# Query blocks outermost, 1536-column exponentials, one gelu block per query block and a planned instruction order in an attention-plus-MLP kernel

## The chip, the cores and the metric

The kernel runs on one core of a Trainium2 chip. The metric is the device time in microseconds (us) of one execution. Every kernel was run several times beside the kernel before on the same chip. The profiled execution's span is about 2 us shorter than its timed run.

## The reference, cut to what matters

```python
x = A_x                                   # (1, 2048, 512), bf16
xn = layernorm(x)                         # no gain, no bias
# attention: 32 heads of 16 columns, no mask
q, k, v = split(xn @ wqkv)
p = softmax(q @ k.T * 16 ** -0.5)         # 32 heads x 2048 x 2048
a = (p @ v) @ wo
# MLP, on a layernorm of the layernorm
y = layernorm(xn)
h = gelu_tanh(y @ w1 + b1)                # 2048 x 1792
out = x + a + (h @ w2 + b2)
```

Softmax needs 32 x 2048 x 2048 = 134 million exponentials. Over 128 lanes that is 1,048,576 columns for ScalarE, whichever way they are cut.

Of the kernel before, what the change touches and what calls it, by code (L numbers as in the profile page):

```python
# [12 lines left out]
ALU = mybir.AluOpType  # L13
# [5 lines left out]
SYNC_DEP = mybir.DependencyInfo(mybir.DependencyClass.Sync, mybir.DependencyReason.DATA)  # L19
# [7 lines left out]
BOUND_INFL = 0.505  # L27
L_MIN = 1e-25
L_MAX = 1e6
GELU_C = float(np.sqrt(2.0 / np.pi))  # L30
_DBG = os.environ.get("PSM_DBG")


class _Jobs:

    NPRIO = 4

    def __init__(self, held):
        self.q = [[] for _ in range(self.NPRIO)]
        self.credit = 0.0  # L40
        self.held = held
        self.sticky = None
        self.activity = 0.0
        self.paused = set()

    def add(self, gen, prio):
        self.q[prio].append(gen)
        return gen

    def _first(self):  # L50
        if self.sticky is not None:
            return self.sticky
        for q in self.q:
            if q and q[0] not in self.paused:
                return q
        return None

    def step(self):
        q = self._first()
        if q is None:  # L60
            return None
        g = q[0]
        try:
            c = next(g)
        except StopIteration:
            q.pop(0)
            c = 0
            assert not self.held(), "job finished while holding the misc bank"
        self.sticky = q if self.held() else None
        if c == "pause":  # L70
            assert self.sticky is None
            self.paused.add(g)
            c = 0
        if isinstance(c, tuple):
            c, a = c
        else:
            a = c
        self.activity += a
        return c

    def run(self, budget):
        self.credit = min(self.credit, 0.0) + budget
        self.activity = 0.0
        self.paused = set()
        while self.credit > 0.0:
            c = self.step()
            if c is None:
                break
            self.credit -= c
        return self.activity  # L90

    def pending(self, gen):
        return any(gen in q for q in self.q)

    def finish(self, gen):
        while self.pending(gen):
            self.paused = set()
            self.step()

    def drain(self):  # L100
        while True:
            self.paused = set()
            if self.step() is None:
                break
        self.credit = 0.0
# [3 lines left out]
def kernel(  # L109
# [11 lines left out]
    dense_per_round: float = 2.4,  # L121
    pe_fill: float = 3.0,
# [13 lines left out]
    NKT = S // P  # L136
    TQ = QW // P
    assert S % QW == 0 and D % P == 0 and F % P == 0 and H % HS == 0
    SW = HS * DH
    NCH = QW // 32  # L140

    const = ctx.enter_context(tc.tile_pool(name="const", bufs=1))
    big = ctx.enter_context(tc.tile_pool(name="big", bufs=1))

    def gate_on(mm, gate):
        if gate is not None:
            tc.add_manual_dep(mm.ins, gate.ins.name, ORDER_DEP, reason="order gate")

# [3 lines left out]
    seln = const.tile([P, P], BF, name="seln")  # L152
    selr = const.tile([P, P], BF, name="selr")
    eps_t = const.tile([P, 1], F32, name="eps_t")
    onescol = const.tile([P, 1], F32, name="onescol")
    onescol2 = const.tile([P, 1], F32, name="onescol2")
    okmin = const.tile([P, 1], F32, name="okmin")
    ones_f = const.tile([P, 1], F32, name="ones_f")
    r2m1 = const.tile([P, NT], F32, name="r2m1")
    b1_sb = const.tile([P, FC], BF, name="b1_sb")  # L160
    b2_sb = const.tile([1, D], BF, name="b2_sb")
    flag_i = const.tile([1, 1], I32, name="flag_i")
    wq_pad = big.tile([P, JC, H, 32], BF, name="wq_pad")
    wk_pad = big.tile([P, JC, H, 32], BF, name="wk_pad")
    wv_sb = big.tile([P, JC, D], BF, name="wv_sb")
    wo_pad = big.tile([P, NS, D], BF, name="wo_pad")
    w1_sb = big.tile([P, JC, F], BF, name="w1_sb")
    w2_sb = big.tile([P, FC, D], BF, name="w2_sb")
    va_bufs = [big.tile([P, NKT, HS, 32], BF, name=f"va{i}") for i in range(2)]
    acc = big.tile([P, NT, D], F32, name="acc")  # L170
    kt0p = big.tile([P, S], BF, name="kt0p")
    kmx0 = const.tile([P, NQT], F32, name="kmx0")
    xnT_c = [big.tile([P, JC, QW], BF, name=f"xnT{tq}") for tq in range(NQT)]
    r2m1b = big.tile([P, S], BF, name="r2m1b")
# [3 lines left out]
    G = 4  # L178

    def load_acc(gate=None):  # L180
        for t0_ in range(0, NT, G):
            d_ = nc.gpsimd.dma_start(acc[:, t0_:t0_ + G, :], xv[:, t0_:t0_ + G, :])
            if gate is not None:
                tc.add_manual_dep(d_.ins, gate.ins.name, SYNC_DEP, reason="x first")

    with tc.tile_pool(name="start", bufs=1) as st, \
            tc.tile_pool(name="startw", bufs=3) as stw, \
            tc.tile_pool(name="pst", bufs=3, space=PSUM) as pst, \
            tc.tile_pool(name="psk", bufs=4, space=PSUM) as psk, \
            tc.tile_pool(name="psw", bufs=1, space=PSUM) as psw:  # L190
        x_sb = st.tile([P, NT, D], BF, name="x_sb")
        for gi_, t0_ in enumerate(range(0, NT, G)):
            (nc.sync if gi_ % 2 == 0 else nc.scalar).dma_start(
                x_sb[:, t0_:t0_ + G, :], xv[:, t0_:t0_ + G, :])
        with nc.allow_non_contiguous_dma(reason="tiny bias load"):
            nc.scalar.dma_start(b1_sb[:], B_b1.rearrange("(fc p) -> p fc", p=P))
        nc.scalar.dma_start(b2_sb[:], B_b2[None, :])

        make_identity(nc, ident_bf[:])
        nc.vector.memset(ones_bf[:], 1.0)  # L200
        nc.vector.memset(zeros_bf[:], 0.0)
        nc.vector.memset(ones_f[:], 1.0)
        nc.vector.memset(seln[:], 0.0)
        nc.vector.memset(selr[:], 0.0)
        for j in range(HS):
            nc.vector.memset(seln[32 * j:32 * j + DH, 32 * j + DH:32 * j + DH + 1], 1.0)
            nc.vector.memset(selr[32 * j:32 * j + 1, 32 * j + DH:32 * j + DH + 2], 1.0)
        nc.vector.memset(eps_t[:], LN_EPS)
        nc.vector.memset(okmin[:], 1.0)
        pm0 = psw.tile([P, 1], F32, tag="w", name="pm0")  # L210
        nc.tensor.matmul(pm0[:], lhsT=selr[:], rhs=ones_bf[:, 0:1], start=True, stop=True)
        nc.vector.tensor_copy(onescol2[:], pm0[:])
        for j in range(HS):
            nc.vector.memset(selr[32 * j:32 * j + 1, 32 * j + DH + 1:32 * j + DH + 2], 0.0)
        pm1 = psw.tile([P, 1], F32, tag="w", name="pm1")
        nc.tensor.matmul(pm1[:], lhsT=selr[:], rhs=ones_bf[:, 0:1], start=True, stop=True)
        nc.vector.tensor_copy(onescol[:], pm1[:])
        for jc in range(JC):
            nc.vector.memset(wk_pad[:, jc, :, DH:32], 0.0)
            nc.gpsimd.memset(wq_pad[:, jc, :, DH:32], 0.0)  # L220
        for va_i in va_bufs:
            nc.gpsimd.memset(va_i[:].rearrange("p k j r -> p (k j r)"), 0.0)
            nc.gpsimd.memset(va_i[:, :, :, DH:DH + 1], 1.0)

        stats = st.tile([P, NT, nc.vector.BN_STATS_DIM], F32, name="stats")
        mv = st.tile([P, NT, nc.vector.BN_AGGR_DIM], F32, name="mv")
        sd1 = st.tile([P, NT], F32, name="sd1")
        sd2 = st.tile([P, NT], F32, name="sd2")
        r1 = st.tile([P, NT], F32, name="r1")
        v2 = st.tile([P, NT], F32, name="v2")  # L230
        assert D <= nc.vector.BN_STATS_FMAX
        gate_stat = None
        for t in range(NT):
            nc.vector.bn_stats(out=stats[:, t, :], in_=x_sb[:, t, :])  # L234
            ag = nc.vector.bn_aggr(out=mv[:, t, :], in_=stats[:, t, :])
            if t == min(NT - 1, 2 * G):
                gate_stat = ag
        wqk = st.tile([P, JC, 2 * D], BF, name="wqk")
        wo_v = A_wo.rearrange("(s j r) c -> j r s c", j=HS, r=DH)
        loads = [(wqk[:, :, D:2 * D], wv_view[:, :, D:2 * D]),  # L240
                 (wqk[:, :, 0:D], wv_view[:, :, 0:D]),
# [3 lines left out]
        for dst_, src_ in loads:  # L245
            d_ = nc.sync.dma_start(dst_, src_)
            tc.add_manual_dep(d_.ins, gate_stat.ins.name, SYNC_DEP, reason="x first")
# [637 lines left out]
```

## The kernel before: the parts that the change and the argument touch

Heads are taken in groups of four ("sets", 8 of them). The loop has the set outermost, then the query block of 512 (`qt`), then the key tile of 128 (`kt`). Each step makes four score tiles (one per head, one PSUM bank each) and two exponentials of two banks.

```python
rounds = [(s, qt, kt) for s in range(NS) for qt in range(NQT) for kt in range(NKT)]
# [cut]
def emit_act(k):
    p_t = ppool.tile([P, 2, QW], BF, tag="p", name=f"p{k}")
    acts[k] = nc.scalar.activation(p_t[:].rearrange("p a b -> p (a b)"),
                                   sct[k][:].rearrange("p a b -> p (a b)"),
                                   AF.Exp, scale=float(DH) ** -0.5)      # 1024 columns
# [cut]
for r in range(NR):
    emit_act(2 * r)
    emit_qk(r + 1)                  # TensorE: next four score tiles
    emit_pv(r - 1)                  # TensorE: P.V of the round before
    done = jobs.run(dense_per_round)        # a budget of other matmuls
    emit_fill(nfill)                # zero matmuls that keep the clock up
    emit_act(2 * r + 1)
```

The other work (projections, MLP, output sums) comes as generator "jobs" that are stepped within a budget in each round, so its place in TensorE's stream follows from the rounds.
The gelu is made of a tanh on ScalarE and three VectorE passes per 512 columns; the division by the softmax sum is done on VectorE with 32x32 transposes; the sums over the sets are kept in an f32 accumulator in SBUF. Both square roots of the layernorms are taken before the stream begins:

```python
nc.scalar.activation(out=sd1[:], in_=mv[:, :, 1], func=AF.Sqrt, bias=eps_t[:], scale=1.0)
# [cut]
nc.scalar.activation(out=sd2[:], in_=v2[:], func=AF.Sqrt, bias=eps_t[:], scale=1.0)
# [cut]
nc.scalar.activation(out=uv, in_=uv, func=AF.Tanh, scale=GELU_C)      # per chunk of 512
```

## Time and profile before

| | before |
|---|---|
| time, median of 4 runs | 1040.63 us (1040.37 to 1042.9) |
| span of the profiled run, mean granted clock | 1038.8 us, 0.986 |
| ScalarE busy | 988.0 us, 95% |
| TensorE busy | 835.0 us, 80% |
| first exponential | 40.2 us |
| last exponential to the end | 12.8 us |

### The profile page before, as it was taken

Reading aid. Unit: us, or ns where it says so; the run is one execution under the profiler, and the core shown is the slowest. Engines: PE = TensorE matmul, PEld = TensorE weight load, DVE = VectorE, ACT = ScalarE, POOL = GpSimd, SP = SyncE. Lnnn points to the kernel's source line nnn. Section 1 sums busy time; section 2 is a strip of 40 time slices with the busy share of each in tenths; the row PEclk is TensorE's granted clock in tenths of the full one; section 3 lists DMA queues with packets and bytes.
Section 4 is the critical chain, followed back from the end, with each engine's and each line's share of the span. In section 5 each row is a group of like instructions: output and inputs, shape, how many; then the busy total and the mean of one; then the engine's idle time right before and its main releaser. Section 6 shows DMA issues by size and latency. Waiting matters only on the chain.

```text
span 1038.8 us, 15620 instructions
## 1 busy us (share of the span) xinstructions
PE 835.0 (80%) x6085; PEld 251.2 (24%) x6197; DVE 452.5 (44%) x976; ACT 988.0 (95%) x1106; POOL 13.2 (1%) x19
## 2 busy tenths in 40 slices
PE   5778877888778889888778887788888877788885
PEld 2312221222212222222222222122222222222221
DVE  8543894513954413536924259451134432112222
ACT  2799999999999999999999999999999999999995
POOL 5000000000000000000000000000000000000000
PEclk8999999999989999999999999999999999999998
DMA  8800000000000000000000000000000000000000
GB/s 256 210 1 1 2 1 1 1 1 1 1 1 1 2 1 1 1 2 1 1 1 1 2 1 1 1 2 1 1 2 1 1 1 1 1 1 21 21 22 23
DMA packets 12913, 15.22 MB, mean 15 GB/s; under 512 B 2337, under 2 KB 10274, under 8 KB 12834
## 3 DMA queue, kind: packets, MB, share of 16 engines
q1 hardware_dynamic: 6704, 7.87, 2.9%
q0 software_dynamic: 2112, 4.19, 1.2%
q10 hardware_dynamic: 4018, 2.10, 0.7%
q8 instruction: 50, 0.82, 0.3%
q14 instruction: 29, 0.24, 0.1%
HBM read 9.97 MB, written 2.10 MB: 12 GB/s over the span
## 4 chain that ended last, share of the span: by engine, by line
ACT 56%; PE 22%; issue 13%; DVE 7%; DMA 1%; ACTq 0%; SPq 0%; DVEq 0%
ACT p L751 53%; PE sc L741 8%; PE o L768 4%; PE o L804 2%; ACT u L598 2%; PE pk L367 1%; PE pq L406 1%; PE po L626 1%; PE ph L580 1%; PE po L607 1%; DVE stats L234 1%; DVE pre L588 1%; DVE qraw L414 1%; PE pvp L476 1%; DMA x_sb<-in_A_x_dram 0%
## 5 line engine op out<-in xcount | busy, mean ns | idle before, releaser
L751 ACT ACTIVATE p<-sc 128x1024 bf16<-128x1024 f32 x1024 | 958.1, 1138 | 14.6 <-PE sc L741 13.2
L768 PE MATMUL o<-p,va 128*32 128x512 bf16 x2048 | 241.1, 391 | 45.7 <-ACT p L751 43.2
L741 PE MATMUL sc<-qt,kt 32*128 32x512 bf16 x1792 | 195.6, 386 | 95.1 <-ACT p L751 87.2
L804 PE MATMUL o<-ones_bf,zeros_bf 128*128 128x512 bf16 x514 | 165.4, 383 | 3.6 <-issue 3.0
L741 PEld LDWEIGHTS <-kt 32*128 32x128 bf16 x1792 | 49.2, 91 | 289.7 <-ACT p L751 265.8
L768 PEld LDWEIGHTS <-va 128*32 128x32 bf16 x2048 | 61.0, 93 | 225.5 <-ACT p L751 116.5
L506 DVE STREAM_TRANSPOSE ta<-o 128x512 f32<-128x512 f32 x32 | 22.9, 716 | 152.8 <-PE o L768 152.8
L580 PE MATMUL ph<-yT,w_sb 128*128 128x512 bf16 x210 | 63.5, 381 | 6.9 <-DVE pre L588 4.8
L632 DVE TENSOR_TENSOR acc<-po,acc 128x512 f32<-128x512 f32 x48 | 33.2, 691 | 77.7 <-PE po L626 69.5
L607 PE MATMUL po<-w_sb,ht 128*128 128x512 bf16 x210 | 63.0, 383 | 3.0 <-issue 1.8
L804 PEld LDWEIGHTS <-zeros_bf 128*128 128x128 bf16 x569 | 45.1, 97 | 72.0 <-issue 54.3
L616 DVE SCALAR_TENSOR_TENSOR acc<-po,acc 128x512 f32<-128x512 f32 x16 | 11.0, 689 | 112.8 <-PE po L613 112.8
L588 DVE TENSOR_SCALAR pre<-ph,b_sb 128x512 f32<-128x512 f32 x56 | 41.8, 747 | 11.8 <-PE ph L580 10.2
L600 DVE SCALAR_TENSOR_TENSOR ht<-u,pre 128x512 bf16<-128x512 f32 x56 | 38.5, 688 | 17.0 <-ACT u L598 16.4
L626 PE MATMUL po<-wo_pad,ont 128*128 128x512 bf16 x118 | 38.1, 389 | 6.6 <-DVE okr L533 2.7
L414 DVE TENSOR_SCALAR qraw<-pq,khalf 128x512 bf16<-128x512 f32 x31 | 23.1, 747 | 46.1 <-PE pq L406 46.1
L598 ACT ACTIVATE u<-u 128x512 f32<-128x512 f32 x56 | 42.5, 760 | 0.0
L374 DVE TENSOR_SCALAR kt<-pk,onescol 128x512 bf16<-128x512 f32 x28 | 20.8, 745 | 43.4 <-PE pk L367 43.4
L367 PE MATMUL pk<-xnT,wk_pad 128*128 128x512 bf16 x104 | 35.6, 403 | 4.7 <-DVE kmx L387 3.5
L592 DVE SCALAR_TENSOR_TENSOR u<-pre 128x512 f32<-128x512 f32 x56 | 38.4, 685 | 1.0
L595 DVE SCALAR_TENSOR_TENSOR u<-u,pre 128x512 f32<-128x512 f32 x56 | 38.4, 685 | 0.9
L406 PE MATMUL pq<-xnT,wq_pad 128*128 128x512 bf16 x115 | 34.7, 382 | 3.1 <-DVE qt L424 1.0
(107 smaller groups left out, 460.0 us busy)
## 6 DMA issues: line engine op xcount, KB each, us to landing
acc<-in_A_x_dram POOLq DMA_DIRECT2D x4, 1024.0 KB, 16.3
w_sb<-in_B_w_dram SPq DMA_DIRECT2D x2, 1792.0 KB, 19.5
x_sb<-in_A_x_dram ACTq DMA_DIRECT2D x2, 512.0 KB, 6.9
x_sb<-in_A_x_dram SPq DMA_DIRECT2D x2, 512.0 KB, 6.3
wqk<-in_A_wqkv_dram SPq DMA_DIRECT2D x2, 512.0 KB, 4.2
out_dram<-ot SPq DMA_DIRECT2D x8, 128.0 KB, 1.7
out_dram<-ot ACTq DMA_DIRECT2D x8, 128.0 KB, 1.7
wv_sb<-in_A_wqkv_dram SPq DMA_DIRECT2D x1, 512.0 KB, 6.2
```

Source lines behind the costliest of these rows:

```text
L367: mm = nc.tensor.matmul(pk[:], lhsT=wk_s[jc], rhs=xnT_c[tq][:, jc, :], start=(jc == 0), stop=(jc == JC - 1))
L406: mm = nc.tensor.matmul(pq[:], lhsT=wq_s[jc], rhs=xnT_c[tq][:, jc, :], start=(jc == 0), stop=(jc == JC - 1))
L580: mm = nc.tensor.matmul(ph[:], lhsT=w1_sb[:, jc, fc * P:(fc + 1) * P], rhs=yT[:, jc, :], start=(jc == 0), stop=(jc == JC - 1))
L588: _Chained.done(nc.vector.tensor_scalar(out=pre[:, fi, :], in0=ph[:], scalar1=b1_sb[:, fc:fc + 1], scalar2=None, op0=ALU.add))
L598: nc.scalar.activation(out=uv, in_=uv, func=AF.Tanh, scale=GELU_C)
L600: nc.vector.scalar_tensor_tensor(out=ht[:, f0 + fi, :], in0=u[:, fi, :], scalar=1.0, in1=pre[:, fi, :], op0=ALU.add, op1=ALU.mult)
L607: mm = nc.tensor.matmul(po[:], lhsT=ht[:, fc, c * P:(c + 1) * P], rhs=w2_sb[:, fc, :], start=(fc == 0), stop=False)
L626: mm = nc.tensor.matmul(po[:], lhsT=ont_tiles[s][:, qs], rhs=wo_pad[:, s, :], start=(i == 0), stop=(i == n - 1))
L741: mm = nc.tensor.matmul(sct[2 * r + j // 2][:, j % 2, :], lhsT=kt_t[lo:lo + 32, kt * P:(kt + 1) * P], rhs=qt_t[lo:lo + 32, qt * QW:(qt + 1 ...
L751: acts[k] = nc.scalar.activation(p_t[:].rearrange("p a b -> p (a b)"), sct[k][:].rearrange("p a b -> p (a b)"), AF.Exp, scale=float(DH) ** ...
L768: mm = nc.tensor.matmul(o_ps[lo:lo + 32, :], lhsT=va_t[:, kt, j, :], rhs=p_t[:, j % 2, :], start=(kt == 0), stop=(kt == NKT - 1), tile_pos ...
L804: nc.tensor.matmul(o_ps[:, :], lhsT=zeros_bf[:, :], rhs=ones_bf[:, :], start=False, stop=False, skip_group_check=True)
```

## The change

The intent: ScalarE should do nothing but exponentials, with fewer fixed costs, from as early as possible, and never wait.

- Query blocks are outermost. All keys and values are built during the first query block and stay in SBUF.
- Exponentials take three PSUM banks (1536 columns): 664 of 1536 and 28 of 1024 in place of 1024 of 1024.
- Gelu is ScalarE's own function, once per query block: two calls of 3584 columns between two table loads. VectorE's three passes are gone.
- All contributions to an output row block (x, w2, bias, wo) are summed in one PSUM bank. Of the eight banks, six hold scores and one the sums of P.V; after the start one "spare bank" is left for all other matmuls in turn.
- The layernorm is done quarter by quarter, by Ln and Exp, so that the stream can start after the first quarter.
- q with 16 columns per head is spread onto 32-row slots by small DMAs, eight per block of eight heads, through two staging buffers `qc`. The sums of the softmax are inverted over a round trip through DRAM.
- The order of every engine's instructions is laid out in advance by a list scheduler. It is given a duration for each operation, and the order is then fixed.

```diff
-rounds = [(s, qt, kt) for s in range(NS) for qt in range(NQT) for kt in range(NKT)]
+units = [(qt, s, k, j) for qt in range(NQT) for s in range(NS) for k in range(NT)
+         for j in range(HS)]
+TILES = ((0, 3), (3, 3))                 # banks of the two score tiles
+EARLY = 56                               # the first 56 alternate three banks and two
+PEN = {1: 0.22, 2: 0.23, 3: 0.25, 4: 0.285}       # planned us of a score or P.V group
+def mmd(n, cols=QW):
+    return n * (cols / 2400.0 + 0.0025)            # planned us of n matmuls
 [cut]
+class _Plan:                             # one op: engine, us, emit, dependences, priority
+    def run(self):                       # repeatedly: of all ready ops, the one that can
+        ...                              # start first; ties within 0.02 us by priority
+    def __call__(self, inst):            # each instruction ordered after the one before it
+        ...
 [cut]
+e = proj("q", misc, key, pr, [...] + list(qc_use.get(n - 2, ())), wq_sb, b, qt, ev, "DVE", dve(QW))
+for par in range(2):
+    def fd(par=par):
+        for j in range(HS):              # four small DMAs
+            lo = 32 * j + DH * par
+            I(nc.sync.dma_start(qz[lo:lo + DH, qt % 2, b, par, :], qc[lo:lo + DH, n % 2, :]))
+    o = add("SP", 0.3, fd, [e, mk_qz[qt % 2]] + [...], pr + par, lat=2.2)
 [cut]
-nc.scalar.activation(out=uv, in_=uv, func=AF.Tanh, scale=GELU_C)
+for h0 in (0, half):
+    hv = ht[:, h0:h0 + half, :].rearrange("p a b -> p (a b)")
+    I(nc.scalar.activation(out=hv, in_=hv, func=AF.Gelu_apprx_tanh, scale=1.0))
 [cut]
-nc.scalar.activation(out=sd1[:], in_=mv[:, :, 1], func=AF.Sqrt, bias=eps_t[:], scale=1.0)
+I(nc.scalar.activation(out=lnv[:, sl], in_=mv[:, sl, 1], func=AF.Ln, bias=eps_t[:], scale=1.0))
+I(nc.scalar.activation(out=r1[:, sl], in_=lnv[:, sl], func=AF.Exp, scale=-0.5))
 [cut]
+I(nc.gpsimd.memset(va[:, t0:t1, :], 0.0))          # GpSimd fills: va, qz, wo_pad
 [cut]
+for f0 in range(0, FC, 3):                         # w2 matmuls of one output block, in threes
+    m = add("PE", mmd(len(fcs)), part(fcs, ...), ...)
+m4 = add("PE", mmd(len(gs) + 1), fin, ...)         # bias and eight wo matmuls in one piece
```

The plan counts a score or P.V group as `PEN`, n other matmuls as `mmd(n)` and four small DMAs as 0.3 us of the issuing queue.

## The prediction

> **What bounds the kernel now.** I read the page first (busy shares, chain, costliest groups), then the waits, then the timeline of ScalarE at the start, in the middle and at the end.
>
> ```profile
> PE 835.0 (80%) x6085; PEld 251.2 (24%) x6197; DVE 452.5 (44%) x976; ACT 988.0 (95%) x1106; POOL 13.2 (1%) x19
> ACT  2799999999999999999999999999999999999995
> ...
> L751 ACT ACTIVATE p<-sc 128x1024 bf16<-128x1024 f32 x1024 | 958.1, 1138 | 14.6 <-PE sc L741 13.2
> L804 PE MATMUL o<-ones_bf,zeros_bf 128*128 128x512 bf16 x514 | 165.4, 383 | 3.6 <-issue 3.0
> L598 ACT ACTIVATE u<-u 128x512 f32<-128x512 f32 x56 | 42.5, 760 | 0.0
> ```
>
> ScalarE is busy 95% of the span and full in 38 of 40 slices. The work is 1024 exponentials of 1024 columns (the softmax) and 56 tanh (the gelu). VectorE at 44% is not the bound, and TensorE's 80% holds 165 us of matmuls with zeros (L804), which only keep its clock up. So the end is set by when ScalarE starts its exponentials, how long its stream lasts, and what follows it.
>
> The ScalarE timeline at the start, in a stretch with one wait, and the last entries of VectorE:
>
> ```profile
> 8.61 1.28 ACT L249 ACT_TABLE_LOAD   x1 [8.61 <-issue]
> 16.64 0.31 ACT L249 ACTIVATE sd<-mv,eps_t 128x16 f32<-128x16 f32 x1 [6.75 <-DVE mv L235]
> 19.55 0.31 ACT L253 ACTIVATE sd<-v,eps_t 128x16 f32<-128x16 f32 x1 [2.60 <-DVE v L252]
> 19.88 1.28 ACT L255 ACT_TABLE_LOAD   x1
> 21.17 0.20 ACT L255 ACTIVATE junk<-sd 128x1 f32<-128x1 f32 x1
> ...
> 40.20 5.61 ACT L751 ACTIVATE p<-sc 128x1024 bf16<-128x1024 f32 x6 [2.21 <-PE sc L741]
> ```
> ```profile
> 817.21 11.11 ACT L751 ACTIVATE p<-sc 128x1024 bf16<-128x1024 f32 x12 [0.38 <-PE sc L741]
> 828.75 14.77 ACT L751 ACTIVATE p<-sc 128x1024 bf16<-128x1024 f32 x16 [0.44 <-PE sc L741]
> ```
> ```profile
> 1026.47 0.72 DVE L506 STREAM_TRANSPOSE ta<-o 128x512 f32<-128x512 f32 x1 [16.09 <-PE o L768]
> ...
> 1032.07 0.69 DVE L637 TENSOR_TENSOR ot<-po,acc 128x512 bf16<-128x512 f32 x1 [0.64 <-DMA out_dram<-ot]
> 1033.11 0.15 DVE L851 CAST flag_i<-cnt 1x1 int32<-1x1 f32 x1 [0.35 <-PE cnt L850]
> ```
>
> The first exponential starts at 40.2. Sixteen in a row take 14.77 us; one that starts after a wait lasts 1.02, so each further one adds (14.77 - 1.02)/15 = 0.917 us. A tanh delays its successor by about 0.51 us. The last exponential ends at 1026.0, and 12.8 us follow: the division of the last head group, its output matmuls, the last sums, and 5.6 us from the cast at 1033.1 to the end. The account of before: 40.2 start + 1024 x 0.917 = 939 exponentials + 56 x 0.51 = 28.5 tanh + 12.8 tail = 1020.5; the 18.3 us left of 1038.8 are waits inside the stream, of the kind seen at 828: TensorE works in order, was in a burst of other matmuls, and delivered scores late.
>
> **What the Trainium skill says.** (1) "ScalarE: Activation LUTs", section "What ACT_TABLE_LOAD costs": an activation with immediates takes 186 ns + 0.833 ns per column and neighbours overlap by 93 ns, so 0.946 us for 1024 columns; the trace has 0.917. The column rate fits, the fixed part is about 0.064 us here. The section also gives 1.28 us for a table load and 1.38 us of drain besides. The trace shows 1.28 (19.88 to 21.17) with the next instruction 0.01 us later, so I count 1.3 us for a switch, not 2.7. (2) Same page, "Table sets: the hidden batching unit": tanh lies in the set of exp, ln and the gelu functions in others (one set has ln and exp together). Before agrees: one load for sqrt, one for exp, none for 56 tanh. (3) "TensorE: Matmul & The Clock Gate", "What's actually happening": the array falls to half clock after an idle window of about 3.4 us and needs a busy one to come back. Here the records show half clock from 15.5 to 25.8 us, after the warming matmuls ended at 11.4.
>
> **The change part by part.** The instruction order of the built kernel gives the counts.
>
> Exponentials: 664 of 1536 columns and 28 of 1024 (the first 56 alternate). At 0.833 ns per column + 0.064 a wide one takes 1.343 us. 664 x 1.343 + 28 x 0.917 = 917.5 us against 939: 21.5 us gained. The gain is only the fixed part of 332 instructions; the columns stay.
>
> Gelu: four blocks, each of a table load, two gelu calls of 3584 columns, and a load back to exp. 0.1 for the finishing exponential + 1.28 + 2 x 3.08 + 1.28 + gaps = 9.0 us, four of them 36 us against 28.5: 7.5 lost. What VectorE loses (three of its four passes per gelu chunk) is off the path.
>
> Start: x arrives in quarters with its layernorm done per quarter by Ln and Exp, and the exponentials start after the first quarter. Landing about 4.2, four statistics at 0.66 to 6.8, Ln 0.31, load 1.28, Exp 0.31 to 8.8, four normalizations and transposes to 11.5, projections at half clock (4 x 0.43 each) with their copies to 16.3; then the order puts a second Ln/Exp pair with two more loads before the first exponential: 19.5 us, against 40.2. 20.7 gained.
>
> Ln/Exp in the stream: the order lists a load before every Ln and before every Exp. Six such pairs (two quarters of the layernorm, four for the second layernorm) lie among the first 28 exponentials. Each costs 0.1 + 2 x 1.28 + 2 x 0.31 and small gaps, 3.4 us; six are 20.4. That is the whole gain of the early start.
>
> VectorE at the start: quarter by quarter it must do statistics (0.66), normalization (0.33), copies of x transposed, K and V from PSUM (about 0.65 each). Walking its order, ScalarE waits about 5 us before the second quarter's pair in the stream and 3 before the third: 8.
>
> TensorE in the stream: the scores of tile i+1 may start when exponential i-1 ends, 1.343 us before they should be followed up. From matmul to exponential takes 0.48 us (0.385 + 0.09), so there are about 0.7 us of slack. Between two tiles of scores the order places bursts, which I cost at 0.2165 us per matmul and 0.33 per group of four P.V. Carrying the delay from tile to tile, the usual burst (P.V and four fillers, 1.2 us) waits nothing, but 16 output blocks have bursts of 1.85 to 2.7 us (seven w2 matmuls; nine of wo and bias), and they cost 21 us together; 2 more for copies of the one spare bank. 23 against 18.3.
>
> Clock: the order places no fillers inside the gelu blocks, so TensorE idles some 8 us there and should fall to half clock; a tile then needs about 2 us of it for some 5 us. About 1.75 us each, 7.
>
> Tail: after the last scores TensorE still has 36 output matmuls to do. From the last exponential: earlier work 1.1, last P.V 0.4, a copy, 23 matmuls 5.0, the final four 0.9, then a copy and four sums at 0.6, and the 5.6 to the end: 16 against 12.8.
>
> Sum with all waits: 19.5 + 917.5 + 36 + 20.4 + 8 + 23 + 7 + 16 = 1047. Without the three kinds of waits (8, 23, 7): 1009.
>
> **Rivals.** (a) It goes as the plan intends: the order was laid out so that ScalarE never waits. The bursts can be shorter than I count where two overlap with slack. Then the floor, 1009 + 2 = 1011 us (the timed runs lie 2 above the span). Against it: the Ln and Exp loads are in the order, and the bursts of 2.7 us also. (b) TensorE becomes the bound: a fixed order that meets slower copies, half clock and late DMA (the division now goes through DRAM) stalls at every set. 30 us more, 1070. Against it: its average is only about 0.3 scores + 0.25 P.V + 0.35 other per 1.343 us, a third of it idle. (c) A table switch costs the page's full 2.66 us: 20 loads x 1.38 = 28 us more. The trace of before speaks against it. (d) The early start is kept whole: if the loads hide behind waits for VectorE, 8 us less than my sum.
>
> **Range and chances.** The walk says 1047, the floor 1009. The burst arithmetic charges every burst in full and the start in series, so I expect less than the sum: 1034 span, 1036 timed, nearly level. A range of 1010 to 1062. 2% faster means below 1019.9, near the floor, 0.23; 2% slower is above 1061.5, 0.16; level 0.61.
>
> **What would show it.** ScalarE's exponentials 1.34 us apart in undisturbed stretches; if 1.30, 27 us less. First exponential near 19.5 and the 28th ended near 79. 24 table loads of 1.28, the next instruction directly behind. Gelu blocks of 9 us with half clock after them. Waits of ScalarE on scores concentrated where output matmuls run, 15 to 30 us in sum. From last exponential to end 16 us. It is wrong if waits of another kind appear (a P.V waiting on a copy, a Q DMA late), or if the loads don't stand in the stream's way.

## The result, and the profile after

| | before | after | predicted |
|---|---|---|---|
| time, median of 4 runs (range) | 1040.63 us (1040.37 to 1042.9) | 1095.42 us (1093.76 to 1097.49) | 1036 (1010 to 1062) |
| ratio, 95% interval | 1 | 1.0524 (1.0504 to 1.0544) | |
| span, mean granted clock | 1038.8 us, 0.986 | 1092.0 us, 0.953 | 1034 |

Ratios are computed as the mean time of one kernel's runs over that of the other's of the same rounds, so they are not quite the ratio of the medians. The changed kernel is 5.2% slower, where the prediction had it nearly level.

The page of the changed kernel, its busy shares, slices and groups, beside the same parts of before in the prediction:

```profile
PE 871.9 (80%) x5841; PEld 284.0 (26%) x5948; DVE 216.0 (20%) x336; ACT 988.8 (91%) x743; POOL 83.9 (8%) x143
...
ACT  1998776999998899999998899999999899999993
...
PEclk9998888999799999998999999999899999999699
...
L842 ACT ACTIVATE p_sb<-ps 128x1536 bf16<-128x1536 f32 (+1 forms) x692 | 927.8, 1604 | 61.0 <-PE ps L823 59.6
```

ScalarE's busy time has not changed (988.0 and 988.8 us): the change put less work in the exponentials and more in loads and gelu. VectorE fell from 452.5 to 216.0 us, which buys nothing here. What is new is the idle time before exponentials that a score matmul ended: 59.6 us, where before had 13.2. The slices say where: the first, and slices 4 to 7 (82 to 191 us), with small dents later. In slices 4 to 7 the granted clock of TensorE is down too (digits of 8).

To size the parts I took the ends of successive exponentials. In an undisturbed stretch they are 1.343 us apart (0.917 for the 1024-column ones); what an interval has above that is called a wait below, and the intervals with a table load in them are counted apart.

| part of the span, us | predicted | measured |
|---|---|---|
| first exponential | 19.5 | 30.7 |
| 664 x 1.343 + 28 x 0.917 | 917.5 | 917.4 |
| four gelu blocks | 36 | 36 (9.0 each) |
| six Ln/Exp pairs in the stream | 20.4 | 18.7 (3.12 each) |
| waits among the first 28 exponentials | 8 | 1.7 |
| waits, exponentials 28 to 90 | 0 (not costed) | 26.4 |
| waits where output matmuls run | 23 | 32.3 (9.7, 9.4, 9.9 and 3.3) |
| waits after the gelu blocks | 7 | 7.8 |
| other small waits | 0 (not costed) | 2.0, and 2.0 beside the loads |
| last exponential to the end | 16 | 16.9 |
| sum | 1047 (1034 chosen) | 1091.9 |

Four views show the new parts. First the start: ScalarE's timeline (start, duration, and in brackets the idle time before with what ended it).

```profile
9.69 0.20 ACT L633 ACTIVATE r<-lnv 128x4 f32<-128x4 f32 x1
14.78 0.59 ACT L664 CAST xnT<-ps 128x512 bf16<-128x512 f32 x1 [4.88 <-PE ps L652]
22.82 0.58 ACT L664 CAST xnT<-ps 128x512 bf16<-128x512 f32 x1 [7.45 <-PE ps L652]
...
30.70 1.43 ACT L842 ACTIVATE p_sb<-ps 128x1536 bf16<-128x1536 f32 x1
```

VectorE and GpSimd in the same stretch:

```profile
9.93 12.07 DVE L643 TENSOR_SCALAR xn_r<-x_sb,mv,r 128x512 bf16<-128x512 bf16 x4 [1.88 <-ACT r L633]
```
```profile
8.82 2.96 POOL L597 MEMSET qz<- 128x3072 bf16 x1
...
18.03 3.51 POOL L602 MEMSET wo_pad<- 128x4096 bf16 x1
```

The scaling factor is there at 9.9 us, 1.1 later than the predicted 8.8. Four normalizations of 512 columns were then predicted at 0.33 us each; they took 12.07 together, beside a row of fills on GpSimd with no gap. ScalarE's waits of 4.88 and 7.45 us are the same time seen from behind two transposes.

Second, the stretch from 150 to 178 us: ScalarE, then VectorE and TensorE, then the queue that issues the DMAs.

```profile
160.35 2.79 ACT L842 ACTIVATE p_sb<-ps 128x1536 bf16<-128x1536 f32 x2 [4.66 <-PE ps L823]
...
174.27 1.45 ACT L842 ACTIVATE p_sb<-ps 128x1536 bf16<-128x1536 f32 x1 [6.50 <-PE ps L823]
```
```profile
157.09 0.69 DVE L735 CAST qc<-ps 128x512 bf16<-128x512 f32 x1 [4.36 <-DMA qz<-qc]
...
170.22 0.94 DVE L902 RECIPROCAL rc<-lc 16x128 f32<-16x128 f32 x1 [7.38 <-DMA lc<-osb]
```
```profile
157.83 1.86 PE L681 MATMUL ps<-xnT,wq_sb 128*128 128x512 bf16 x4 [3.38 <-DVE qc L735]
```
```profile
123.27 2.44 SPq L745 DMA_DIRECT2D qz<-qc  x4
...
127.77 38.62 SPq L745 DMA_DIRECT2D qz<-qc  x36
166.50 2.53 SPq L896 DMA_DIRECT2D lc<-osb  x4
```

Read it from ScalarE backwards. ScalarE waits 4.66 us for scores. The scores stand behind a q projection, which waits 3.38 us for the spare bank until VectorE has copied the q before. VectorE waits 4.36 us for a DMA out of a staging buffer. And the queue was issuing small DMAs, 2.44 us for four where the plan had 0.3. (The row of 36 hides one pause: single starts in the trace show the queue standing from 130.2 to 145.2 us, then 32 DMAs in a row until 166.4.)

The longer wait, 6.50 us, comes by another path from the same queue. There the q projection waited 6.35 us, since VectorE's next copy of q stood behind a reciprocal, and that waited 7.38 us for the softmax sums. Their DMAs (`lc<-osb`) were issued at 166.50, behind the q DMAs, though their data had been ready since 158.4. And the wait of 3.70 us at 133.50 follows a VectorE wait of 4.14 us for the inverted sums on their way back from DRAM. The plan counts four copies of sums as 0.25 us, and they take 2.53 us to issue.

Third, a stretch with output matmuls. ScalarE, and TensorE just before the second of these waits:

```profile
347.64 6.82 ACT L842 ACTIVATE p_sb<-ps 128x1536 bf16<-128x1536 f32 x5 [1.35 <-PE ps L823]
356.28 6.82 ACT L842 ACTIVATE p_sb<-ps 128x1536 bf16<-128x1536 f32 x5 [1.82 <-PE ps L823]
```
```profile
352.44 0.39 PE L823 MATMUL ps<-qz,kt 32*128 32x512 bf16 x3
352.76 0.40 PE L865 MATMUL ps<-p_sb,va 128*32 128x512 bf16 x4
353.09 0.61 PE L1073 MATMUL ps<-w_sb,ht 128*128 128x512 bf16 x2
353.63 0.39 PE L1088 MATMUL ps<-b_sb,ones_bf 1*128 1x512 bf16 x1
353.95 1.90 PE L1091 MATMUL ps<-wo_pad,ont 128*128 128x512 bf16 x8
355.78 0.60 PE L823 MATMUL ps<-qz,kt 32*128 32x512 bf16 x6
```

The scores wait behind two w2 matmuls, the bias and the eight wo matmuls, from 353.09 to 355.78 = 2.7 us, and ScalarE pays 1.82 for it. This is the burst the prediction had in mind. The starts also give what TensorE needs for a group: 0.32 us for three score matmuls and 0.33 for four of P.V (352.44, 352.76, 353.09); the plan had 0.25 and 0.285.

Fourth, a gelu block on ScalarE:

```profile
267.79 1.28 ACT L1049 ACT_TABLE_LOAD   x1
269.08 6.27 ACT L1049 ACTIVATE ht<-ht 128x3584 bf16<-128x3584 bf16 x2
275.37 1.28 ACT L842 ACT_TABLE_LOAD   x1
276.66 4.13 ACT L842 ACTIVATE p_sb<-ps 128x1536 bf16<-128x1536 f32 x3
```

Load, two gelu, load, next exponential, with 0.01 to 0.02 us between them: the block is what was predicted.

### The profile page after: what moved, and what is told of

It is laid out like the page before. It is cut to its first block, busy times and chain, and to the rows that moved or that the text cites. A ratio compares the mean times of both kernels' runs of the same rounds, so it can differ in the third digit from the quotient of the medians.

```text
span 1092.0 us, 14577 instructions
## 1 busy us (share of the span) xinstructions
PE 871.9 (80%) x5841; PEld 284.0 (26%) x5948; DVE 216.0 (20%) x336; ACT 988.8 (91%) x743; POOL 83.9 (8%) x143
## 4 chain that ended last, share of the span: by engine, by line
ACT 47%; PE 26%; issue 18%; DVE 5%; SPq 3%; DMA 1%; DVEq 0%; ACTq 0%
ACT p_sb L842 43%; PE ps L823 6%; PE ps L1073 4%; PE ps L1035 4%; PE ps L865 4%; PE ps L1173 3%; PE ps L1091 2%; SPq L745 2%; DVE ht L1040 1%; ACT ht L1049 1%; PE ps L681 1%; DVE xn_r L643 1%; SPq L896 1%; DMA lc<-osb 1%; ACT L842 0%
## 5 line engine op out<-in xcount | busy, mean ns | idle before, releaser
L842 ACT ACTIVATE p_sb<-ps 128x1536 bf16<-128x1536 f32 (+1 forms) x692 | 927.8, 1604 | 61.0 <-PE ps L823 59.6
L823 PE MATMUL ps<-qz,kt 32*128 32x512 bf16 x2048 | 273.4, 391 | 152.7 <-ACT p_sb L842 143.3
L1173 PE MATMUL ps<-ones_bf,zeros_bf 128*128 128x512 bf16 x893 | 260.6, 395 | 11.7 <-issue 11.7
L865 PE MATMUL ps<-p_sb,va 128*32 128x512 bf16 x2048 | 207.2, 397 | 0.1
L823 PEld LDWEIGHTS <-kt 32*128 32x128 bf16 x2048 | 87.5, 91 | 404.2 <-issue 393.9
L1035 PE MATMUL ps<-yT,w_sb 128*128 128x512 bf16 x214 | 58.7, 389 | 5.8 <-DVE ht L1040 5.0
L1073 PE MATMUL ps<-w_sb,ht 128*128 128x512 bf16 x208 | 54.9, 381 | 1.0 <-issue 0.3
L1040 DVE TENSOR_SCALAR ht<-ps,b_sb 128x512 bf16<-128x512 f32 x56 | 41.9, 749 | 63.7 <-PE ps L1035 63.3
L902 DVE RECIPROCAL rc<-lc 16x128 f32<-16x128 f32 x31 | 29.2, 941 | 99.4 <-DMA lc<-osb 99.4
L916 DVE TENSOR_TENSOR ont<-osb,rlb 128x512 bf16<-128x512 f32 x31 | 21.5, 692 | 130.8 <-DMA rlb<-rdram 130.8
L1091 PE MATMUL ps<-wo_pad,ont 128*128 128x512 bf16 x124 | 29.5, 381 | 0.0
L1035 PEld LDWEIGHTS <-w_sb 128*128 128x128 bf16 x224 | 20.0, 98 | 31.6 <-issue 16.9
L681 PE MATMUL ps<-xnT,wq_sb 128*128 128x512 bf16 x57 | 17.8, 435 | 11.5 <-DVE qc L735 10.8
L652 PE MATMUL ps<-ident_bf,xn_r 128*128 128x128 bf16 x64 | 7.0, 249 | 22.8 <-DVE xn_r L643 22.4
L681 PE MATMUL ps<-xnT,wkv 128*128 128x512 bf16 x61 | 19.5, 439 | 4.3 <-DVE kt L697 3.1
```

What stands on the lines that cost most here:

```text
L681: I(nc.tensor.matmul(ps[:, bk, :], lhsT=w[:, jc, b * P:(b + 1) * P], rhs=xnT[:, qt, jc, :], start=(jc == 0), stop=(jc == JC - 1)))
L823: I(nc.tensor.matmul(ps[:, b0 + x, :], lhsT=kt[lo:lo + 32, s // 2, k * P:(k + 1) * P], rhs=qz[lo:lo + 32, qt % 2, s // 2, s % 2, :], start ...
L842: I(nc.scalar.activation(p_sb[:, s0:s1, :].rearrange("p a b -> p (a b)"), ps[:, b0:b0 + n, :].rearrange("p a b -> p (a b)"), AF.Exp, scale ...
L865: I(nc.tensor.matmul(ps[32 * j:32 * j + 32, OB, :], lhsT=va[:, k, h * VS:h * VS + 32], rhs=p_sb[:, unit_slot[u0 + j], :], start=(c == 0), ...
L902: I(nc.vector.reciprocal(rc[:, i2, :], lc[:, i2, :]))
L1035: I(nc.tensor.matmul(ps[:, bk, :], lhsT=w1_sb[:, jc, fc * P:(fc + 1) * P], rhs=yT[:, jc, :], start=(jc == 0), stop=(jc == JC - 1)))
```

## The experiments

The theory after the first look: the arithmetic of ScalarE's own work was right, and the 58 us between 1034 and 1092 are waits of four kinds: (1) GpSimd's fills against VectorE at the start, (2) the small DMAs of q in the 28th to 90th exponential, (3) TensorE's work where the outputs are summed, (4) half clock after gelu. The rival for all of them is that a part taken away is only refilled by another wait, since ScalarE's stream has a fixed order. All kernels below gave correct results. "Before" was 1039.9 to 1041.3 us in all their rounds.

| run | what | median us (range) | ratio to before (95%) |
|---|---|---|---|
| e1_pool_late | fills after the first quarter's normalizations | 1092.58 (1087.74 to 1092.79) | 1.048 (1.0448 to 1.0512) |
| e1b_fills_away | fills out of the way of all normalizations | 1087.36 (1086.38 to 1092.93) | 1.0467 (1.0437 to 1.0498) |
| e2_mask_q | q by masks, no small DMAs, first form | 1090.2 (1085.03 to 1091.83) | 1.046 (1.0424 to 1.0496) |
| e2b_mask_q | the same, with the projection placed later | 1081.02 (1079.93 to 1081.99) | 1.0388 (1.0371 to 1.0405) |
| e2c_qc3 | three staging buffers | 1095.57 (1092.8 to 1097.75) | 1.0524 (1.0496 to 1.0552) |
| e2d_dma_cost | plan told 2.45 us for four DMAs | 1076.77 (1076.11 to 1077.94) | 1.035 (1.033 to 1.0369) |
| e2cd_both | both of these | 1074.61 (1071.74 to 1075.52) | 1.0319 (1.0294 to 1.0343) |
| e3_short_bursts | output matmuls in pieces of two or three | 1088.6 (1086.92 to 1090.04) | 1.0461 (1.0439 to 1.0483) |
| e8_pe_cost | plan told TensorE's measured costs | 1085.17 (1084.11 to 1087.72) | 1.0424 (1.0399 to 1.045) |
| e7_short_true_pe | both of these | 1075.46 (1070.61 to 1076.36) | 1.0322 (1.0293 to 1.035) |
| e9_both_costs | plan told both measured costs, nothing else | 1072.42 (1070.92 to 1072.56) | 1.0293 (1.0272 to 1.0314) |
| e4_fill_gelu | zero matmuls in the gelu gaps | 1089.6 (1088.81 to 1092.51) | 1.0471 (1.0444 to 1.0497) |
| e5_r2_once | second layernorm's Ln/Exp once | 1090.39 (1087.2 to 1093.51) | 1.0476 (1.0447 to 1.0506) |
| all6b | e1, e2b, e3, e4, e5 and TensorE's costs | 1042.04 (1040.8 to 1043.27) | 1.0013 (0.9997 to 1.003) |
| all9 | the same with the fills of e1b | 1028.91 (1024.57 to 1030.53) | 0.9879 (0.985 to 0.9907) |
| all10 | all9 and a shorter end | 1018.9 (1016.03 to 1022.12) | 0.9789 (0.976 to 0.9818) |
| all11_w1024 | all10 with 1024 columns | two fast: 1042.62, 1045.65 | unclear |

### The start: fills beside normalizations

**e1_pool_late.** All big fills but the first wait for the first quarter's fourth normalization.

```diff
+            g_ = I(nc.gpsimd.memset(va[:, t0:t1, :], 0.0))
+            if t0 == 4:        # the first of the late fills; the others follow it in order
+                tc.add_manual_dep(g_.ins, xn_inst[3].ins.name, SYNC_DEP, reason="after xn")
```

> The big GpSimd memsets (the second to fourth quarter of va, qz, wo_pad) wait for the fourth normalization of the first quarter. Theory (the normalizations, bf16 from SBUF, were locked out[...] while GpSimd filled): four normalizations take 1.5 us instead of 12.07, the first exponential comes near 20.5 us instead of 30.7, and about 8 to 10 us of that reach the end: 1085 to 1088 us. Rival (the start is set by the arrival of x or by TensorE at half clock): normalizations still late, first exponential after 28, time within 2 us of 1095.

Measured: the first exponential started at 19.3 in place of 30.7 us, the predicted 19.5. But the time fell by only 2.8 us, and the waits among the first 28 exponentials rose from 1.7 to 9.5. VectorE's timeline says why: the fills had moved under the second quarter.

```profile
21.85 7.22 DVE L654 TENSOR_SCALAR xn_r<-x_sb,mv,r 128x512 bf16<-128x512 bf16 x2
```

So the fills are the cause of the late start, and the same collision happens wherever they stand beside a normalization.

**e1b_fills_away.** GpSimd fills only the pad columns of `va` before x lands, and `qz` and `wo_pad` after the last normalization.

```diff
-            I(nc.gpsimd.memset(va[:, t0:t1, :], 0.0))
+            I(nc.gpsimd.memset(vh[:, :, :, DH + 1:VS], 0.0))       # pads only
+            I(nc.gpsimd.memset(va[:, t0:t1, H * VS:], 0.0))
 [cut]
+            tc.add_manual_dep(g_.ins, xn_inst[NT - 1].ins.name, SYNC_DEP, reason="after xn")
```

> Against the changed kernel, GpSimd fills only the pad columns of va (16 of 18 columns per head are overwritten anyway) at the start, and qz and wo_pad after the last normalization. In the run with late fills the second quarter's four normalizations took 10 us beside fills that had only been moved. Theory (a fill on GpSimd shuts the bf16 normalizations out as long as it runs): no group of four normalizations over 2 us in any quarter, first exponential near 19.5, 28th ended at 70 to 73 instead of 81.7, time 1083 to 1087. Rival (the start is bound by the sum of VectorE's work): the 28th ends after 77, time above 1089.

```profile
9.58 1.38 DVE L654 TENSOR_SCALAR xn_r<-x_sb,mv,r 128x512 bf16<-128x512 bf16 x4 [1.88 <-ACT r L644]
```

Four normalizations take 1.38 us in place of 12.07. The Trainium skill's page "SBUF — State Buffer", section "Who interferes with whom", says that VectorE and GpSimd share a pair of ports, that a VectorE copy or tensor_scalar in a two-port mode takes the pair for a whole instruction, and that the later one "fully blocks". This agrees: 12.07 us beside fills, 1.38 without, and in e1_pool_late a copy out of PSUM at 21.26 us took its usual 0.67 beside a fill. The 28th exponential ended at 75.1 in place of 81.7 us; the kernel is 8 us faster by its medians, not 11.7, because the waits among the first 28 rose to 6.2: part of the gain of an earlier start was only waiting moved.

### The 26 us: q blocks

**e2_mask_q** and **e2b_mask_q.** The halves of q are made by two VectorE multiplications with a 0/1 mask straight from PSUM; the copy, the staging buffers and the 120 small DMAs are gone.

```diff
-        e = proj("q", misc, key, pr, [...], wq_sb, b, qt, ev, "DVE", dve(QW))     # copy to qc
-                    I(nc.sync.dma_start(qz[lo:lo + DH, qt % 2, b, par, :], qc[lo:lo + DH, n % 2, :]))
+                I(nc.vector.tensor_scalar(out=qz[:, qt % 2, b, par, :], in0=ps[:, misc.bank(key), :],
+                                          scalar1=mask[:, par:par + 1], scalar2=None, op0=ALU.mult))
```

> Every q block is split into its two zero-padded halves by VectorE with the masks (two passes of about 0.7 us from PSUM, as the first block already is) instead of one copy and eight small DMAs. Theory (between 80 and 180 us TensorE waits behind q projections whose bank is not emptied because the copies wait for DMAs issued at 0.6 us each): the waits of the exponentials between 80 and 200 us fall from about 26 us to under 6, time 1071 to 1077. Rival (those waits come from TensorE at half clock or having too much to do there): they stay above 18, time above 1088.

> As the mask run before, which moved its waits: there the q matmul of a later block took the one spare bank in the planned order and its copy then waited for the old block's scores, and four output blocks were planned in lumps of 23 matmuls. Here the q matmul itself waits for those scores. Theory (the waits of exponentials 28 to 90, 26 us, come from q blocks held up by small DMAs): they are 8 us or less and nothing is added elsewhere, time 1072 to 1078. Rival (only moved about): waits over the whole stream stay above 48 us, time above 1086.

The first form took the waits in the stretch from 26.4 to 6.1 us, but the time fell by only 5.2: the planner now started a projection as soon as its inputs were there, which held the one spare bank until the old q block was no longer read, and all other work came in lumps later (waits of 18 us in the first output stretch in place of 9.7). e2b makes the projection wait for the old block's last scores. Then the waits are 6.2 us and the time is 14.4 us lower. That shows that the q blocks are the place, but three things went at once: the DMAs, the two buffers, and a cost in the plan.

**e2c_qc3, e2d_dma_cost, e2cd_both** take these apart.

```diff
-    qc = const.tile([P, 2, QW], BF, name="qc")
+    qc = const.tile([P, 3, QW], BF, name="qc")            # e2c, with n % 3 and qc_use.get(n - 3)
```
```diff
-            o = add("SP", 0.3, fd, [e, mk_qz[qt % 2]] + [...])
+            o = add("SP", 2.45, fd, [e, mk_qz[qt % 2]] + [...])      # e2d: only the plan's cost
```

> Three staging buffers of q in place of two, nothing else. If the two buffers made the waits (VectorE's copy waits for a buffer, TensorE for VectorE), the waits between the 28th and the 90th exponential fall from 26 us to 12 or less and the time by 10 us or more, to below 1086. If the issue of the small DMAs (some 0.6 us each, 2.4 us per half group) is the cause, a third buffer only fills up a little later: the waits stay above 18 us and the time at 1088 to 1096.

> The planner is told 2.45 us for the four small DMAs of half a head group in place of 0.3; the kernel's operations are the same, only their order changes. If the waits come from an order that was laid out with the wrong cost, they fall from 26 to 12 us or less, since the order then asks for q when it is there. If the rate of the small DMAs is the cause whatever the order, they stay above 18 us.

> Three staging buffers and the true cost of the DMAs in the plan together. If buffers or plan or the two together are the cause, waits between the 28th and the 90th exponential come to 8 us or less and the time to 1075 to 1081, as with the masks (1081 with 6 us of such waits). If the issue rate is the cause, the waits stay above 18 us and only the masks help.

A third buffer alone changed nothing: 25.4 us of waits, 1095.57 us. One constant in the plan, with not one operation changed, took the waits to 7.3 us and the time down by 18.6 us, more than removing the DMAs had. (The order changed in other places too: the first gelu block now comes before the 89th exponential in place of the 150th.) With it ScalarE runs through the same stretch:

```profile
136.40 16.23 ACT L842 ACTIVATE p_sb<-ps 128x1536 bf16<-128x1536 f32 x12 [0.42 <-PE ps L823]
153.79 14.88 ACT L842 ACTIVATE p_sb<-ps 128x1536 bf16<-128x1536 f32 x11 [1.17 <-PE ps L823]
```

So the issue rate of the small DMAs is not a limit by itself. The order asked for q blocks faster than the queue could deliver them, because the plan thought the queue eight times as fast. Both together gave 8.9 us of waits in the stretch and 2 us off e2d, so the buffer is worth little even then. The rival, that the issue rate keeps the waits above 18 us, fitted e2c and fell with e2d and e2cd. Not tested are the plan's costs of the softmax sums' DMAs, which stayed at 0.25 us for four in every version; they may be in the 5 to 9 us that remain.

### The output stretches: length and load

**e3_short_bursts.** The eight wo matmuls and the bias come in pieces of two, the w2 matmuls in twos.

```diff
-            for f0 in range(0, FC, 3):
+            for f0 in range(0, FC, 2):
 [cut]
-            m4 = add("PE", mmd(len(gs) + 1), fin, ...)
+            for n0 in range(0, len(gs), 2):
+                m4 = add("PE", mmd(n1 - n0 + (n0 == 0)), fin(n0, n1), ...)
```

> The output matmuls are handed to the planned order in pieces of two or three instead of three and nine. No burst between two tiles of scores over 1.8 us (before 27 bursts of 1.8 to 2.7). Theory (the waits in the four output stretches, about 9.5 us each in the first three and 6 in the last, come from the length of the bursts): they fall to 2 us each or less, time 1067 to 1075. Rival (they come from waiting for copies of the one spare bank or from the sum of the work): they stay over 6 us per stretch, time over 1088.

Measured: 10.0, 8.1 and 7.6 us of waits in the three stretches in place of 9.7, 9.4 and 9.9. By that, burst length alone is refuted as the whole cause: the large waits went, but many small ones took their place.

**e7_short_true_pe** and **e8_pe_cost** give the planner the measured costs of TensorE, with the short pieces and without.

```diff
-    PEN = {1: 0.22, 2: 0.23, 3: 0.25, 4: 0.285}
+    PEN = {1: 0.32, 2: 0.32, 3: 0.325, 4: 0.33}
-        return n * (cols / 2400.0 + 0.0025)
+        return n * (cols / 2400.0 + 0.0025) + 0.1
```

> Short pieces as in the run with short bursts, and the planner is told the measured durations of TensorE's groups (0.325 and 0.33 us for a group of scores and of P.V, 0.1 more for a chain of others) instead of 0.25 and 0.285. The planned order then holds about 1.2 us of TensorE per exponential in the output stretches instead of 1.59 (changed kernel) and 1.40 (short bursts). Theory (the stretches are TensorE-bound because the plan was packed to costs that are too small): waits of each of the three output stretches fall from 9.7 (8.6 with short bursts) to under 3, time 1064 to 1072. Rival (copies of the one spare bank): they stay above 6, time above 1082.

> Only the planner's costs of TensorE change (a score group 0.32 us in place of 0.25, P.V 0.33 in place of 0.285, 0.1 more for each chain of matmuls); the bursts keep their lengths of up to nine matmuls. If the plan packed too much work per exponential because its costs were too low, the three output stretches fall from 9.7, 9.4 and 9.9 us to 2 to 4 each and the time to 1075 to 1082, with a tail longer by some 6 us. If the length of a burst matters as well (a wait of its own for each piece over about 0.7 us of slack), 5 to 8 us stay in each and the time is 1084 to 1092.

Pieces and costs together: 1.8, 2.2 and 3.2 us, and a run of 25 exponentials without a wait where the changed kernel had four (its tail grew by 6 us, since work was put off to the end). Costs alone: 8.5, 7.5 and 6.8 us. So each is needed and neither suffices. The load shows in TensorE's busy time over the same 20 exponentials, from the start of the 190th to that of the 210th, where the first output blocks are summed (columns: window, length, busy with instruction count, clock, DMA share, GB/s). First the changed kernel, then e8, then e7:

```profile
333.50:367.26 33.76, 33.08 (x215) 1.00 0.09 26
```
```profile
333.28:364.27 30.99, 30.86 (x205) 1.00 0.07 23
```
```profile
332.88:360.04 27.16, 26.83 (x184) 1.00 0.05 15
```

TensorE spent 33.08/20 = 1.65 us per exponential in the changed kernel, 1.54 in e8 and 1.34 in e7; in e3 it was 1.50 (29.90 us). ScalarE takes 1.343. So the waits go with the load, and only both edits together bring it down to what fits. In e8 the load alone accounts for them: 20 x (1.54 - 1.343) = 4.0 us, and ScalarE waited 4.1 there. Why the order still holds more than fits when the plan has the measured costs and the pieces are undivided is not shown; and since e3's shorter pieces lowered the load too, what the length does by itself is not separated. The copies of the spare bank are no cause of their own: e7 kept them, and its waits nearly went.

**e9_both_costs** has the two corrections of the plan's costs together and no changed operation.

> Both corrections of the plan's costs together (TensorE's and the four small DMAs'), no operation changed. If the two act on different stretches and add, 18.6 us of the DMAs and what the TensorE costs alone give: 1057 to 1064. If the one refills the other's gain, 1068 or more.

1072.42 us: 23.0 less than the changed kernel, where the two gave 18.6 and 10.3 alone. The sum was not reached. Part of it was counted twice: TensorE's costs alone had already taken the waits between the 28th and 90th exponential from 26.4 to 20.7 us. And 7.4 us of new waits stand between the 90th and 149th. So the rival "refilled by another wait" holds in part.

### Gelu gaps and the second layernorm

**e4_fill_gelu** lets the plan fill gaps over 4 us with zero matmuls.

```diff
-            if recent >= FILL * 3.4:
+            if recent >= FILL * 3.4 and t1 - t0 < 4.0:
```

> The planned gap of some 9 us in TensorE during each gelu block is filled with matmuls with zeros. Theory (the waits of 1.5 to 2.6 us after each gelu block, 6 to 7 us in sum, come from half clock): clock 1.0 in and after the four blocks, these waits gone, time 1088 to 1090. Rival (they come from the refill of the pipeline): the waits stay, time within 1 us of 1095.

```profile
268.16 10.10 PE L1173 MATMUL ps<-ones_bf,zeros_bf 128*128 128x512 bf16 x45
278.20 0.39 PE L823 MATMUL ps<-qz,kt 32*128 32x512 bf16 x3
```

The first scores after the block took 0.39 us in place of 0.61. The granted clock, 0.5 from 270.0 to 283.7 us in the changed kernel, is 1.0 here from 267 to 290 us, and its mean rose from 0.953 to 0.976. The waits after three of the gelu blocks fell from 2.6, 1.5 and 2.7 to 0, 1.1 and 0, which is 5.7 us. The median fell by 5.8, but that the two agree is chance: between the profiled runs the span fell by 3.7 and the waits in sum by 3.3, since other waits grew. Half clock after gelu is a cause, of the predicted size, and part of it was refilled.

**e5_r2_once** takes the second layernorm's four Ln/Exp pairs together in one.

```diff
-        b = add("ACT", 0.5, fl, (a,), lo - 10)             # one pair per query block
+        if qt == 0:
+            r2_all.append(add("ACT", 0.5, fl, (a,), lo - 10))      # all 16 columns at once
+        b = r2_all[0]
```

> The Ln and Exp of the second layernorm are done once for all four blocks, so three of the six pairs in the stream and six table loads go. Theory (each pair costs the stream 3.12 us): the 28th exponential ends 9.4 us earlier, near 72.3, time 1084 to 1087. Rival (the pairs lie where ScalarE would wait anyway): the time they leave is filled with waits, 28th near 80, time within 3 us of the changed kernel (about 1092).

Three pairs of 3.12 us are gone (9.4 us), and the 28th exponential ended 3.9 us earlier, at 77.8; the time fell by 5.0 us. Part of the rest was refilled: the waits from 28 to 90 rose to 29.3.

### All together

**all6b** has e1, e2b, e3, e4, e5 and TensorE's costs; **all9** has the fills of e1b in place of those of e1; **all10** also shortens the end: for the last query block, six of the eight head groups are summed ahead and the last two at the end.

```diff
-                pr = ts_(qt, NS - 1) + 8 + 4 * c
-                gs = gs[:-1]
+                pr = ts_(qt, NS - 2) + 8 + 4 * c
+                gs = gs[:-2]
```

> All together: late GpSimd fills, q by masks, short pieces with measured TensorE costs, gelu gaps filled, second layernorm once. Taking the waits as independent, from 1092 of the profile: start 3, q 20, second layernorm 9, output stretches 22, gelu gaps 5: 1033 of span, 1035 timed, level with the kernel before (1041) or a little faster. If they hide each other (a wait taken away only shows the next), above 1060.

> All together, with the fills out of the way (qz needs none with the masks). Theory: the one wait of 9 us in the second quarter of the joint run goes, 28th exponential ended by 69 instead of 77, time 1031 to 1036 against 1042. Rival: other waits of the start take its place, time above 1039.

> As all9, and the last block's sums take in six of its eight head groups ahead and only the last two at the end, so that the 23-matmul chains need not be finished after the last exponential. Tail 21.7 us in the joint run; expected 14 to 16, time 1024 to 1030, 1 to 1.6% faster than the kernel before.

all6b is level with before at 1042.04 us. Its waits among the first 28 were 14.2 us, the fills beside the second quarter again; all9 has 2.2 there, ends its 28th exponential at 63.9 in place of 77.0 us and takes 1028.91. In both the tail was 22 us. all10 has 12.7 and takes 1018.9 us: the version that beats both kernels, before by 2.1% (faster clear of noise, but the interval, 0.976 to 0.9818, holds 2%, so the verdict at that threshold is unclear) and the kernel under study by 7% (1018.9/1095.42). Its page:

```profile
PE 876.2 (86%) x5949; PEld 279.5 (27%) x5949; DVE 215.4 (21%) x345; ACT 975.4 (96%) x731; POOL 69.7 (7%) x145
...
ACT  5999989999999999999999999999999999999995
...
L847 ACT ACTIVATE p_sb<-ps 128x1536 bf16<-128x1536 f32 (+1 forms) x692 | 923.3, 1605 | 17.4 <-PE ps L828 16.5
```

The idle time that scores ended is 16.5 us, near the 13.2 of before, and ScalarE is full from the second slice to the 39th but for one.

**all11_w1024** puts 1024-column exponentials into all10, to see what the width by itself is worth.

```diff
-    TILES = ((0, 3), (3, 3))
+    TILES = ((0, 2), (2, 2), (4, 2))
 [cut]
```

> all10 with exponentials of 1024 columns in three double banks instead of 1536 in two triple banks: the price of the width alone, in the best version. From the measured 0.917 and 1.343 us the stream gets 21.5 us longer; three tiles in flight leave more slack, so waits may shrink by up to 10. Expected 12 to 22 us above all10. If the width is worth nothing, within 4 us.

Its profiled run, a fast one, has a span of 1040.8 us against 1018.2: 22.6 us, where the fixed part of 332 instructions gives 21.5. Two of its runs were fast (1042.62 and 1045.65); the other two are marked slow (1063.56 and 1067.78) and are not used, and the verdict on the timed runs stays unclear. The spans agree with the arithmetic of one instruction; start, tail and waits differ by under 2 us each between the two profiles.

## Why the prediction was wrong

Taken by its own steps:

1. **Exponentials, gelu, table loads, tail: right.** 1.343 us per wide exponential (measured 1.343), 9.0 us per gelu block (9.0), 3.4 per Ln/Exp pair (3.12), loads of 1.28 with the next instruction directly behind (so rival (c) fell), tail 16 (16.9). Half clock after gelu was charged with 7 us and cost 7.8; e4 took most of it away by filling the gaps. The gain from the width, the fixed part of 332 instructions, is real: all11 gives 22.6 us where 21.5 were predicted.

2. **First exponential at 19.5: wrong by 11.2 us.** The step "four normalizations and transposes to 11.5" assumed 0.33 us each. They took 12.07 us together beside GpSimd's fills. The prediction walked VectorE's order and never looked at what GpSimd does meanwhile, and the profile of before had GpSimd at 1%. Without the collision the start is 19.0 to 19.6 us (e1, e1b, all10). It cost less than 11.2 in the end, since the 8 us of start waits shrank to 1.7: the 28th exponential ended at 81.7, 2.7 us later than the predicted 79. That nearness is luck, two errors against each other: with the fills out of the way (e1b) the start waits are 6.2 us.

3. **Waits inside the stream: the failed step.** The prediction added 8 at the start, 23 for bursts and copies, and 7 for the clock: 38 us. Measured are 70 (1.7 + 26.4 + 32.3 + 7.8 + 2.0). Two terms failed:
   - *Nothing was charged for the stretch in which the q blocks are built; it cost 26.4 us.* Its list of what would make it wrong named "a Q DMA late", but the DMAs were never costed: 2.44 us per four on the issuing queue, against 0.3 in the plan. e2d shows the plan's constant to be the cause of 19.1 of the 26.4: the same operations in an order made with 2.45 leave 7.3. e2c shows that the two staging buffers were not the cause.
   - *Bursts were charged with 21 us and 2 for copies; the output stretches cost 32.3.* The single bursts were sized well: 1.36, 1.35, 1.82 and 1.49 us of idle time in the first stretch, against 21/16 = 1.3, and the waits of over 1.2 us in the four stretches sum to 22.4. The other 9.9 us are smaller waits, where the prediction had 2. What was missed is the load: from the 190th to the 210th exponential TensorE worked 1.65 us per exponential of 1.343. The prediction had found TensorE a third idle on average; in the places where work was packed it was not. e3, e8 and e7 show that both the pieces and the plan's costs had to be mended.

4. **The discount from 1047 to 1034** was an opinion ("charges every burst in full and the start in series"). The bursts did cost their full price. Without it the miss would have been 45 us rather than 58.

5. **Rival (b), TensorE as the bound, "a fixed order that meets slower copies, half clock and late DMA", 1070 us,** was the nearest, and was set aside because TensorE's average load is two thirds. That argument is the error in method: an engine that works in a fixed order is a bound wherever the order is locally too dense or waits for something that the plan has wrong, whatever its average. The rival's late DMA was that of the division, and this DMA does stand in the path of two of the long waits (3.70 and 6.50 us); the q DMAs, which fill the same queue, it did not have, and the stalls did not come at every set.

What stays open: where the new waits of e9 between the 90th and 149th exponential come from; why the order of e8 still holds more than fits; whether all10 would be faster still with the q DMAs at their measured cost in place of the masks (e2d was faster than e2b; not tried); and the 5 to 9 us of waits that stay between the 28th and 90th exponential in the mended versions.

## What to carry to other kernels

When an order is fixed in advance, predict from the durations that the planner was given: put each beside a measured one, the DMA issues first, since one constant that was eight times too small cost 18.6 us here. Judge an in-order engine by its load in the densest stretch per step of the engine it feeds (here 1.65 us for 1.343), not by its average. And before moving fills or other setup to an "idle" engine, see what the neighbour that shares its ports does at that time.

## What the Trainium skill lacked or had wrong

- "ScalarE: Activation LUTs", section "What ACT_TABLE_LOAD costs": it gives 1.28 us and 1.38 us of drain for each switch. The load agrees (1.28); no drain shows. The next instruction follows 0.01 to 0.02 us after a load, and a whole gelu block with two switches costs 9.0 us, where two drains would add 2.8.
- "DMA: Bandwidth & Descriptors", section "Issuing engines are not separate DMA queues": it calls the time to initiate a DMA on the sequencer "usually small relative to the DMA itself" and gives no figure for it there. It was a cost that the plan had to have right. The trace gives the issue of one of the 16 KB transfers of q as min/median/max in ns, and 32 of them in a row held the queue from 145.2 to 166.4 us:

```profile
L745 SPq DMA_DIRECT2D qz<-qc x120: 507/575/1843, 29.2 to 569.8; - x120
```

- No page has the time from one small group to the next where score groups and P.V groups alternate as here. Medians of the traces, from start to next start: 0.325 us for four score matmuls of 32 rows each (kernel before), 0.323 for three (changed kernel), 0.333 for a P.V group of four (changed kernel). So three score matmuls in place of four save TensorE nothing per group.
